# Gated attention products of batches 2 to 7 computed with the gated values stationary and 512 weight columns moving

## The chip, the cores and the metric

The kernel runs on one core of a Trainium2 chip. The time of a kernel is the device time of one execution in microseconds (us); a comparison takes the median of several. The five engines are called as the profile calls them: PE is TensorE (matmuls; PEld are its loads of the stationary operand), DVE is VectorE, ACT is ScalarE, POOL is GpSimd, and SP (SyncE) issues the transfers.

## What is computed

The reference, cut to its core:

```python
q_s = softmax of q over d;  k_s = softmax of k over s         # q, k, v: (8, 8, 576, 64)
kv = np.einsum('bhsd,bhse->bhde', k_s, v)
attn = np.einsum('bhsd,bhde->bhse', q_s, kv)
x = attn.transpose(0, 2, 1, 3).reshape(8, 576, 512)
gate_pre = sum(conv_w[k] * xp[:, k:k + S, :] for k in range(5))   # causal, along s
gate = 1.0 / (1.0 + np.exp(-gate_pre))
val = x @ w_val                                                # 512 x 512
return gate * val @ w_out                                      # 512 x 512
```

There are 8 batches of 576 tokens with 512 channels. The two products with the 512 x 512 weights, val and out, are most of the arithmetic.

## The kernel before

Everything of a batch lies with channels on the partitions, in four blocks of 128 channels, and with the 576 tokens as columns. A batch goes through these steps, each a function that the list ORDER calls by name with the batch and a block: the softmax of q and k (steps q_..., k_..., l_..., c_...), kv (L484), attend (L543: x, two blocks at a time), x_high and x_low (x as a sum of two fp32r parts), first, tap, far and near (the five taps of the convolution, on ACT, DVE, and POOL), sigmoid (L580), value (val), gated (L652: g = gate times val), g_high (gh, a rounded copy of g, L168 on ACT or L170 on POOL and DVE), g_low (gl = g - gh, L660, mostly on POOL), project (out), copy (half of out from the PSUM buffer to o, L174 on ACT or L178 on DVE) and put (L680: the transfer of o to memory).

ORDER has been written out by hand and is executed word for word (the schedule is manual): every engine gets its instructions in the order of the list, and only waits move them in time. Steps of neighbouring batches are interleaved; around the products of batch b stand the attend, taps and x parts of batch b+1 and the softmax of batches b+2 and b+3.

Value and project use split_product (L593). A step "project b n" makes output channels of block n: for each of the 4 input blocks there are three parts, gh with the low and the high half of the weights and gl with the high half; the weights' 128 x 128 block is stationary, and the tokens move in two halves of 288 columns. That is 12 parts x 2 halves = 24 matmuls, each with a load of weights. Of the block that gated made last, all three parts come at the end.

The PSUM holds four buffers of 128 x 1024 (tag "bank"), which x, val, out and others take in the order of the list; the first matmul into a buffer waits until its last reader is done. gh and gl have four buffers each, o has two.

Of the kernel before, what the change touches and what calls it, by code (L numbers as in the profile page):

```python
# [23 lines left out]
STAGED = 6  # L24
EPS = 1e-9
# [32 lines left out]
    q_turned 1 1 a, g_high 0 3 a, first 1 0 a, g_low 0 3 p, signed 6, load_k 2, first 1 1 a, tap 1 0 3, tap 1 0 1,
    load_q 3 0 5, tap 1 1 3, joined 6 p, project 0 1, x_high 1 0 a, w_high 6 a, tap 1 0 0, tap 1 1 0, copy 0 1 a a,
    k_spread 2, x_high 1 1 a, tap 1 0 2, q_sub 2 4 p, project 0 0, x_low 1 0, w_low 6 p, load_km 6 2, tap 1 1 1,  # L60
    put 0 1, attend 1 1, q_sub 2 3 p, copy 0 0 a a, part 7 a, tap 1 1 2, x_high 1 3 a, load_vt 2, signed 7,
    x_low 1 1, load_vt 4, q_sub 2 2 p, joined 7 p, first 1 2 a, q_sub 2 0 p, x_low 1 3, x_high 1 2 a, q_sub 2 1 p,
    load_km 4 1, project 0 2, far 1 2 2, x_low 1 2, load_km 4 2, w_high 7 a, load_v 2, w_low 7 p, tap 1 2 1,
    q_max 3 0 4, value 1 0, k_sub 2 1 p, q_sub 3 1 p, load_km 3 3, tap 1 2 3, k_sub 2 4 p, sigmoid 1 0, first 1 3 a,
    copy 0 2 a a, project 0 3, q_exp 2 0 5, gated 1 0, q_sum 2 0 5, k_peak 3 0, kt_exp 2, q_sub 3 0 p, q_eps 2 0 5 a,
    k_sub 2 3 p, tap 1 3 0, load_km 5 3, value 1 1, put 0 0, copy 0 3 a a, q_rec 2 0 5, k_sub 2 0 p, tap 1 3 2,
    tap 1 3 1, tap 1 3 3, k_sub 2 2 p, k_peak 3 3, q_mul 2 3 p, value 1 3, load_km 3 1, g_high 1 0 p, tap 1 2 0,
# [689 lines left out]
```

## Time and profile before

| | |
|---|---|
| median of 3 runs | 288.77 us (288.74 to 289.95) |
| span of the profiled execution | 287.3 us, 1.5 us below the median |
| busy PE | 267.8 us, 93% |
| busy DVE | 231.5 us, 81% |
| busy POOL | 206.2 us, 72% |
| busy ACT | 191.6 us, 67% |
| matmuls | 2616, of them 744 with 128 x 288 columns of out_a, and 24 of the two halves of the last product |

The span lies between the first and the last instruction; what the run has beside it, start and end, is the 1.5 us. Busy shares are averages over the whole span. The chain of waits goes back from the last instruction to what released each step; a step with a line and a count is so many instructions one behind the other on that engine. In a timeline each row is a start, a duration of the run of equal instructions, and the idle time before it where there was one. Matmuls overlap, so a group's mean duration is longer than their spacing.

### The profile page before, as it was taken

Reading aid. Unit: us, or ns where it says so; the run is one execution under the profiler, and the core shown is the slowest. Engines: PE = TensorE matmul, PEld = TensorE weight load, DVE = VectorE, ACT = ScalarE, POOL = GpSimd, SP = SyncE. Lnnn points to the kernel's source line nnn. Section 1 sums busy time; section 2 is a strip of 40 time slices with the busy share of each in tenths; the row PEclk is TensorE's granted clock in tenths of the full one; section 3 lists DMA queues with packets and bytes.
Section 4 is the critical chain, followed back from the end, with each engine's and each line's share of the span. In section 5 each row is a group of like instructions: output and inputs, shape, how many; then the busy total and the mean of one; then the engine's idle time right before and its main releaser. Section 6 shows DMA issues by size and latency. Waiting matters only on the chain.

```text
span 287.3 us, 6606 instructions
## 1 busy us (share of the span) xinstructions
PE 267.8 (93%) x2616; PEld 248.2 (86%) x2616; DVE 231.5 (81%) x332; ACT 191.6 (67%) x323; POOL 206.2 (72%) x187
## 2 busy tenths in 40 slices
PE   0198999999999999999999999999999999999995
PEld 0075799889998899889999898999989898989995
DVE  2999899999979999899669989799659774759610
ACT  2799999977797668856956773688945733645002
POOL 3767968989999986899898993879379193533300
PEclk9999999999999999999999999999999999999999
DMA  7999894598379899969997969645645700112022
GB/s 232 385 412 417 329 332 114 190 332 322 117 164 285 298 259 346 349 223 233 368 411 246 235 232 343 256 164 131 178 149 149 217 8 2 43 41 82 2 82 82
DMA packets 23462, 62.92 MB, mean 219 GB/s; under 512 B 3432, under 2 KB 3976, under 8 KB 20744
## 3 DMA queue, kind: packets, MB, share of 16 engines
q1 hardware_dynamic: 23432, 62.51, 65.5%
q8 instruction: 20, 0.33, 0.5%
q14 instruction: 10, 0.08, 0.1%
HBM read 52.96 MB, written 9.54 MB: 218 GB/s over the span
## 4 chain that ended last, share of the span: by engine, by line
PE 65%; DVE 13%; DMA 8%; POOL 6%; ACT 4%; issue 3%; SPq 0%; DVEq 0%; POOLq 0%; ACTq 0%
PE out_a L593 31%; PE val L593 25%; PE x L543 4%; DMA kc<-in_k_channels 4%; PE kv L484 3%; DMA kt<-in_k_tail 3%; POOL gl L660 2%; DVE gate L568 2%; DVE ktop L339 1%; ACT q L469 1%; DMA words<-in_w_val 1%; POOL q L471 1%; DVE g L652 1%; DVE e L263 1%; DVE qs L393 1%
## 5 line engine op out<-in xcount | busy, mean ns | idle before, releaser
L593 PE MATMUL val<-x,w_val_hi 128*128 128x288 f32 x512 | 89.0, 295 | 0.0
L568 DVE SCALAR_TENSOR_TENSOR gate<-x,cw,gate 128x575 f32<-128x575 f32 (+3 forms) x98 | 78.3, 808 | 4.8 <-ACT gate L556 1.9
L593 PEld LDWEIGHTS val<-x,w_val_hi 128*128 128x128 f32 x512 | 75.2, 188 | 0.1
L593 PE MATMUL val<-x,w_val_lo 128*128 128x288 f32 x256 | 56.0, 300 | 0.1
L593 PE MATMUL out_a<-gh,w_out_lo 128*128 128x288 f32 x248 | 54.6, 301 | 0.2 <-ACT far L573 0.2
L593 PE MATMUL out_a<-gh,w_out_hi 128*128 128x288 f32 x248 | 53.2, 296 | 0.0
L660 POOL TENSOR_TENSOR gl<-g,gh 128x576 fp32r<-128x576 f32 x25 | 36.1, 1443 | 13.8 <-ACT gh L168 6.5
L593 PEld LDWEIGHTS out_a<-gh,w_out_lo 128*128 128x128 f32 x248 | 39.3, 188 | 5.7 <-issue 2.2
L593 PE MATMUL out_a<-gl,w_out_hi 128*128 128x288 f32 x248 | 43.1, 295 | 0.3 <-POOL gl L660 0.3
L593 PEld LDWEIGHTS val<-x,w_val_lo 128*128 128x128 f32 x256 | 40.7, 188 | 1.4 <-issue 0.6
L577 POOL TENSOR_TENSOR gate<-gate,far 128x572 f32<-128x572 f32 (+3 forms) x22 | 29.0, 1320 | 16.4 <-DVE gate L568 8.1
L593 PEld LDWEIGHTS out_a<-gh,w_out_hi 128*128 128x128 f32 x248 | 39.8, 188 | 0.0
L383 POOL TENSOR_TENSOR q<-q,qm 128x512 f32<-128x512 f32 x32 | 32.9, 1044 | 6.3 <-DVE qm L378 6.3
L593 PEld LDWEIGHTS out_a<-gl,w_out_hi 128*128 128x128 f32 x248 | 36.4, 188 | 0.6 <-POOL gl L660 0.6
L174 ACT ACTIVATE o<-out_a 128x576 f32<-128x576 f32 x26 | 16.9, 651 | 29.3 <-PE out_a L593 22.6
L652 DVE SCALAR_TENSOR_TENSOR g<-gate,val 128x576 f32<-128x576 f32 x32 | 23.9, 750 | 15.4 <-PE val L593 10.1
L453 POOL TENSOR_TENSOR qc<-qc,lb 128x576 f32<-128x576 f32 (+1 forms) x17 | 24.3, 1439 | 10.8 <-DMA lb<-lrow 8.2
L318 POOL TENSOR_TENSOR k<-k,kmax 128x512 f32<-128x512 f32 x23 | 30.1, 1328 | 0.2
L580 ACT ACTIVATE gate<-gate 128x576 f32<-128x576 f32 x30 | 20.1, 682 | 8.6 <-DVE gate L568 7.1
L563 DVE TENSOR_TENSOR x<-x,x 128x576 fp32r<-128x576 f32 x32 | 23.2, 749 | 1.7 <-ACT x L168 1.6
L573 ACT ACTIVATE far<-x,cw 128x572 f32<-128x572 f32 (+3 forms) x22 | 16.2, 739 | 12.5 <-PE x L543 4.7
L168 ACT CAST x<-x 128x576 fp32r<-128x576 f32 x27 | 17.0, 640 | 7.3 <-PE x L543 4.2
(110 smaller groups left out, 441.2 us busy)
## 6 DMA issues: line engine op xcount, KB each, us to landing
out<-o SPq DMA_DIRECT2D x31, 288.0 KB, 3.9
v<-in_v SPq DMA_DIRECT2D x8, 1040.0 KB, 8.7
q<-in_q SPq DMA_DIRECT2D x7, 1024.0 KB, 8.6
km<-in_k_strided SPq DMA_DIRECT2D x24, 288.0 KB, 5.5
k<-in_k SPq DMA_DIRECT2D x6, 1024.0 KB, 8.5
qc<-in_q_channels SPq DMA_DIRECT2D x16, 288.0 KB, 7.7
lb<-lrow SPq DMA_DIRECT2D x8, 576.0 KB, 5.9
kc<-in_k_channels SPq DMA_DIRECT2D x8, 288.0 KB, 6.9
```

The costliest lines, as they stand in the source:

```text
L168: nc.scalar.copy(out=out, in_=in_)
L174: nc.scalar.mul(out, in_, factor)
L318: engine(e).tensor_sub(kk[r, cs], kk[r, cs], mx[r, cs])
L383: engine(e).tensor_tensor(qq, qq, m, op=ALU.add if b < 2 else ALU.subtract)
L453: engine(e).tensor_sub(t, t, T["lb", b][:, p])
L563: nc.vector.tensor_sub(xl, T["x", b, p], T["xh", b, p].bitcast(F32))
L568: nc.vector.scalar_tensor_tensor(out=a, in0=x, scalar=w, in1=a, op0=ALU.mult, op1=ALU.add)
L577: nc.gpsimd.tensor_add(a, a, T["far", b, p, j])
L580: nc.scalar.activation(T["gate", b, p], T["gate", b, p], AF.Tanh, scale=0.5)
L593: nc.tensor.matmul(ps[:, cs], a[:, kb, ms], z[:, cs], start=(i == 0), stop=(i == len(parts) - 1))
L652: nc.vector.scalar_tensor_tensor(out=T["g", b, m], in0=T["gate", b, m], scalar=1.0, in1=T["val", b, m], op0=ALU.add, op1=ALU.mult)
L660: engine(e).tensor_sub(T["gl", b, m], T["g", b, m], T["gh", b, m].bitcast(F32))
```

## The change

Batches 0 and 1 stay as they are. From batch 2 on (FIRST_TURNED) the product of project is made the other way round: 128 tokens of gh or gl are the stationary operand, and 512 columns of weights move, so that a step makes 128 tokens with all 512 output channels. Steps n = 0 to 3 are the first 512 tokens, with 12 matmuls of 512 columns instead of 24 of 288. The last 64 tokens of a batch go into a shared tile gt of its pair (batches 2 and 3, 4 and 5, 6 and 7): g_high and g_low copy and subtract them in an instruction of 64 columns of their own, while gh and gl have 512 columns now. A new step "project b 4" of the odd batch makes the product of the 128 tail tokens of the pair, again 12 matmuls, with a copy and a put of its own. The last product, project 7 3, stays split in two halves, now of 256 output channels. The output array is flat, its bytes are the same, and the host brings it into the reference's shape.

The functions:

```diff
     def g_high(b, m, e="a"):
-        T["gh", b, m] = block("gh", f"gh_{b}_{m}", 4, F32R)
-        copied(e, T["gh", b, m], T["g", b, m])
+        T["gh", b, m] = block("gh", f"gh_{b}_{m}", 4, F32R, columns(b))
+        copied(e, T["gh", b, m], T["g", b, m][:, :columns(b)])
+        if turned(b):
+            copied(e, g_tails(b)[:, 0, m, rows(b)], T["g", b, m][:, MAIN:])
 
     def g_low(b, m, e="p"):
-        T["gl", b, m] = block("gl", f"gl_{b}_{m}", 4, F32R)
-        engine(e).tensor_sub(T["gl", b, m], T["g", b, m], T["gh", b, m].bitcast(F32))
+        T["gl", b, m] = block("gl", f"gl_{b}_{m}", 4, F32R, columns(b))
+        engine(e).tensor_sub(T["gl", b, m], T["g", b, m][:, :columns(b)], T["gh", b, m].bitcast(F32))
+        if turned(b):
+            hi, lo = (g_tails(b)[:, i, m, rows(b)] for i in range(2))
+            engine(e).tensor_sub(lo, T["g", b, m][:, MAIN:], hi.bitcast(F32))
+
+    def turned(b):
+
+        return b >= FIRST_TURNED
+
+    def columns(b):
+        return MAIN if turned(b) else S
+
+    def g_tails(b):
+        if ("gt", b // 2) not in T:
+            t = pair(f"gt_{b // 2}", F32R, "late", 2)[:, :2 * NB * P]
+            T["gt", b // 2] = t.rearrange("p (i n s) -> p i n s", i=2, n=NB)
+        return T["gt", b // 2]
 
     def project(b, n, h="a"):
+        if turned(b):
+            return token_product(b, n, h)
         T["out", b, n, h] = halved_bank(f"out_{b}_{n}_{h}")
         split_product(T["out", b, n, h], W[1], blocks("gh", b), blocks("gl", b), n, T["gates", b], 1, h)
 
-    def piece(h):
+    def token_product(b, n, h="a"):
+
+        cs = piece(b, h)
+        ps = T["out", b, n, h] = bank(f"out_{b}_{n}_{h}")[:, :MAIN]
+        if n < 4:
+            hi, lo = ([t[:, n * P:n * P + P] for t in blocks(x, b)] for x in ("gh", "gl"))
+        else:
+            hi, lo = ([g_tails(b)[:, i, kb] for kb in range(NB)] for i in range(2))
+        wh, wl = W[1]
+        order = T["gates", b]
+        parts = []
+        for ks in (order[:NB - 1], order[NB - 1:]):
+            parts += [(hi[kb], w, kb) for kb in ks for w in (wl, wh)] + [(lo[kb], wh, kb) for kb in ks]
+        for i, (a, w, kb) in enumerate(parts):
+            nc.tensor.matmul(ps[:, cs], a, w[:, kb, cs], start=(i == 0), stop=(i == len(parts) - 1))
+
+    def piece(b, h):
+        if turned(b):
+            return cols(h)
         ts = tokens(h)
         return slice(ts[0].start, ts[-1].stop)
 
     def copy(b, n, h, e):
         if ("o", b, n) not in T:
             T["o", b, n] = block("o", f"o_{b}_{n}", 2)
-        cs = piece(h)
+        cs = piece(b, h)
         mid = (cs.start + cs.stop) // 2
         for i, k in enumerate(e):
             c = cs if len(e) == 1 else (slice(cs.start, mid), slice(mid, cs.stop))[i]
             times(k, T["o", b, n][:, c], T["out", b, n, h][:, c], 0.5)
 
     def put(b, n, h="a"):
-        nc.sync.dma_start(out=out[b, n][:, piece(h)], in_=T["o", b, n][:, piece(h)])
+        cs = piece(b, h)
+        to = out.rearrange("(t p j) -> t p j", p=P, j=C)[36 // 8 * b + b // 2 + n] if turned(b) else out.rearrange("(t p j) -> t p j", p=P, j=S)[b * NB + n]
+        nc.sync.dma_start(out=to[:, cs], in_=T["o", b, n][:, cs])
```

In ORDER steps are added and one is moved (put 3 1 stood before x_low 5 0). The list's lines are cut here to the steps around each place:

```diff
-    near 4 1 1, k_exp 5, k_peak 7 3, project 3 2, q_sub 6 3 p,
+    near 4 1 1, k_exp 5, k_peak 7 3, project 3 2, project 3 4, q_sub 6 3 p,
...
-    copy 3 2 a a, tap 4 2 2, put 3 2, l_sub 5 1 p, load_qc 6 1, kv 5,
+    copy 3 2 a a, tap 4 2 2, put 3 2, copy 3 4 a a, put 3 1, put 3 4, l_sub 5 1 p, load_qc 6 1, kv 5,
...
-    first 5 2 a, put 3 1, x_low 5 0,
+    first 5 2 a, x_low 5 0,
...
-    put 5 1, project 5 3, load_qc 7 0,
+    put 5 1, project 5 3, project 5 4, load_qc 7 0,
...
-    copy 5 3 a a, first 6 2 v, sigmoid 6 0, put 5 3, tap 6 2 3,
+    copy 5 3 a a, copy 5 4 a a, first 6 2 v, sigmoid 6 0, put 5 3, put 5 4, tap 6 2 3,
...
-    put 7 1, project 7 3 r, copy 7 2 a a, put 7 2, project 7 3 l,
+    put 7 1, project 7 4, project 7 3 r, copy 7 2 a a, copy 7 4 a v, put 7 2, put 7 4, project 7 3 l,
```

There are 744 + 24 matmuls of out before; of them 576 belong to batches 2 to 7, and 336 take their place. The 24 tail copies are on ACT (9), POOL (11) and DVE (4), the 24 tail subtractions on POOL (17) and DVE (7); there are three more copies of out (two on ACT, one on DVE) and three more puts.

On PE, the end of project 3 2 and the start of value 4 0, which comes behind it; before:

```order
L593 MATMUL out_3_2_a_2259<-gh_3_3_2119,w_out_lo_80 128x288 x2
L593 MATMUL out_3_2_a_2259<-gh_3_3_2119,w_out_hi_79 128x288 x2
L593 MATMUL out_3_2_a_2259<-gl_3_3_2125,w_out_hi_79 128x288 x2
L593 MATMUL val_4_0_2301<-x2_4_0_2121,w_val_lo_78 128x288 [waits DVE_49]
L593 MATMUL val_4_0_2301<-x2_4_0_2121,w_val_lo_78 128x288
L593 MATMUL val_4_0_2301<-x2_4_0_2121,w_val_hi_77 128x288 x2
L593 MATMUL val_4_0_2301<-x2_4_1_2204,w_val_lo_78 128x288 x2
L593 MATMUL val_4_0_2301<-x2_4_1_2204,w_val_hi_77 128x288 x2
```

and with the change:

```order
L702 MATMUL out_3_2_a_2192<-w_out_hi_79,gh_3_3_2086 128x512
L702 MATMUL out_3_2_a_2192<-w_out_hi_79,gl_3_3_2093 128x512
L702 MATMUL out_3_4_a_2205<-w_out_lo_80,gt_1_1498 128x512 [waits DVE_49,PE_49]
L702 MATMUL out_3_4_a_2205<-w_out_hi_79,gt_1_1498 128x512
L702 MATMUL out_3_4_a_2205<-w_out_lo_80,gt_1_1498 128x512
L702 MATMUL out_3_4_a_2205<-w_out_hi_79,gt_1_1498 128x512
L702 MATMUL out_3_4_a_2205<-w_out_lo_80,gt_1_1498 128x512
L702 MATMUL out_3_4_a_2205<-w_out_hi_79,gt_1_1498 128x512 x4
L702 MATMUL out_3_4_a_2205<-w_out_lo_80,gt_1_1498 128x512
L702 MATMUL out_3_4_a_2205<-w_out_hi_79,gt_1_1498 128x512
L702 MATMUL out_3_4_a_2205<-w_out_hi_79,gt_1_1498 128x512 [waits Pool_49]
L595 MATMUL val_4_0_2235<-x2_4_0_2089,w_val_lo_78 128x288 [waits Activation_49]
```

Twelve matmuls of 512 columns with the tail tile gt as stationary operand stand between the two products; the first of them waits for DVE, which val 4 0 did before, and val 4 0 waits for ACT.

On ACT, from the copy of out 3 1 (o_3_1) to the exp of q of batch 6; k5 is the exp of k, gate_4_0 and gate_4_1 are the two sigmoids; before:

```order
L174 ACTIVATE o_3_1_2254<-out_3_1_a_2207 128x576 [waits DMAHW7_49,PE_49,Activation_49]
L322 ACTIVATE k5_1883<-k5_1883 128x2048 [waits DMAHW0_49,Pool_49]
L168 CAST x2_4_3_2285<-x_4_3_2244 128x576 [waits PE_49]
L556 ACTIVATE gate_4_3_2293<-x_4_3_2244,cw_76 128x576
L580 ACTIVATE gate_4_0_2152<-gate_4_0_2152 128x576 [waits DVE_49]
L580 ACTIVATE gate_4_1_2191<-gate_4_1_2191 128x576 [waits DVE_49,Pool_49]
L174 ACTIVATE o_3_2_2329<-out_3_2_a_2259 128x576 [waits DMAHW2_49,PE_49,Activation_49]
L387 ACTIVATE q6_2044<-q6_2044 128x2560 [waits DMAHW0_49,Pool_49]
```

and with the change:

```order
L176 ACTIVATE o_3_1_2187<-out_3_1_a_2152 128x512 [waits DMAHW7_49,PE_49,Activation_49]
L324 ACTIVATE k5_1844<-k5_1844 128x2048 [waits DMAHW0_49,Pool_49]
L170 CAST x2_4_3_2219<-x_4_3_2177 128x576 [waits PE_49]
L558 ACTIVATE gate_4_3_2227<-x_4_3_2177,cw_76 128x576
L582 ACTIVATE gate_4_0_2109<-gate_4_0_2109 128x576 [waits DVE_49]
L582 ACTIVATE gate_4_1_2136<-gate_4_1_2136 128x576 [waits DVE_49,Pool_49]
L176 ACTIVATE o_3_2_2263<-out_3_2_a_2192 128x512 [waits DMAHW2_49,PE_49,Activation_49]
L176 ACTIVATE o_3_4_2267<-out_3_4_a_2205 128x512 [waits DMAHW4_49,PE_49,Activation_49]
L389 ACTIVATE q6_2007<-q6_2007 128x2560 [waits DMAHW0_49,Pool_49]
```

The copy of out 3 2 stands at the same place behind the exp and the two sigmoids, and the copy of out 3 4 comes behind it.

On POOL, the last gh and gl of batch 2 ahead of project 2 0; before:

```order
L170 CAST gh_2_3_1676<-g_2_3_1581 128x576 [waits DVE_49]
L660 TENSOR_TENSOR gl_2_3_1678<-g_2_3_1581,gh_2_3_1676 128x576 [waits PE_49,Pool_49]
L660 TENSOR_TENSOR gl_2_0_1700<-g_2_0_1549,gh_2_0_1673 128x576 [waits PE_49,Activation_49]
L170 CAST gh_2_2_1703<-g_2_2_1689 128x576 [waits DVE_49]
L660 TENSOR_TENSOR gl_2_2_1706<-g_2_2_1689,gh_2_2_1703 128x576 [waits PE_49,Pool_49]
L453 TENSOR_TENSOR qc_3_2_1543<-qc_3_2_1543,lb3_1448 128x512 [waits DMAHW5_49]
```

and with the change:

```order
L172 CAST gh_2_3_1680<-g_2_3_1584 128x512 [waits DVE_49]
L172 CAST gt_1_1498<-g_2_3_1584 128x64
L664 TENSOR_TENSOR gl_2_3_1683<-g_2_3_1584,gh_2_3_1680 128x512 [waits PE_49,Pool_49]
L667 TENSOR_TENSOR gt_1_1498<-g_2_3_1584,gt_1_1498 128x64 [waits Pool_49]
L664 TENSOR_TENSOR gl_2_0_1706<-g_2_0_1552,gh_2_0_1676 128x512 [waits PE_49,Activation_49]
L667 TENSOR_TENSOR gt_1_1498<-g_2_0_1552,gt_1_1498 128x64 [waits Activation_49]
L172 CAST gh_2_2_1710<-g_2_2_1695 128x512 [waits DVE_49]
L172 CAST gt_1_1498<-g_2_2_1695 128x64
L664 TENSOR_TENSOR gl_2_2_1714<-g_2_2_1695,gh_2_2_1710 128x512 [waits PE_49,Pool_49]
L667 TENSOR_TENSOR gt_1_1498<-g_2_2_1695,gt_1_1498 128x64 [waits Pool_49]
L455 TENSOR_TENSOR qc_3_2_1545<-qc_3_2_1545,lb3_1448 128x512 [waits DMAHW5_49]
```

Each gh and gl of 576 columns has become one of 512 and one of 64 on the shared tile gt.

## Rows read from the trace of the kernel before

**Rows 1.** The page: busy PE, and DVE and clock in 40 slices of 7.18 us.

```profile
PE 267.8 (93%) x2616; PEld 248.2 (86%) x2616; DVE 231.5 (81%) x332; ACT 191.6 (67%) x323; POOL 206.2 (72%) x187
...
DVE  2999899999979999899669989799659774759610
...
PEclk9999999999999999999999999999999999999999
```

**Rows 2.** Chain of waits from 118 us: start in us, length, engine and line.

```profile
121.74 1.44 POOL gl L660
...
123.22 3.73 PE out_a L593 x26
126.95 1.29 PE x L543 x16
128.23 6.59 PE out_a L593 x48
...
161.23 1.13 PE x L543 x16
162.37 3.39 PE out_a L593 x24
165.76 3.20 PE val L593 x24
...
182.55 3.20 PE out_a L593 x24
```

**Rows 3.** Groups by line, matmul and load: shapes, count, busy us, mean ns, idle.

```profile
L593 PE MATMUL out_a<-gh,w_out_lo 128*128 128x288 f32 x248 | 54.6, 301 | 0.2 <-ACT far L573 0.2
...
L593 PEld LDWEIGHTS out_a<-gh,w_out_lo 128*128 128x128 f32 x248 | 39.3, 188 | 5.7 <-issue 2.2 <-ACT o L174 1.8 <-DVE g L652 0.9
```

**Rows 4.** Timeline of PE: start, us, engine, line, tiles, shapes, count.

```profile
87.74 0.82 PE L509 MATMUL qTps<-ident,q 128*128 128x128 f32 x6
```

**Rows 5.** Timeline of DVE in 121 to 134.5 us.

```profile
125.33 1.65 DVE L568 SCALAR_TENSOR_TENSOR gate<-x,cw,gate 128x573 f32<-128x573 f32 x2
...
130.48 1.41 DVE L563 TENSOR_TENSOR x<-x,x 128x576 fp32r<-128x576 f32 x2
```

**Rows 6.** Timeline of DVE in 159 to 160 us.

```profile
159.10 1.53 DVE L568 SCALAR_TENSOR_TENSOR gate<-x,cw,gate 128x572 f32<-128x572 f32 x2
```

**Rows 7.** Timeline of ACT in 161.9 to 167 us.

```profile
161.99 1.92 ACT L322 ACTIVATE k<-k 128x2048 f32<-128x2048 f32 x1
...
164.97 1.26 ACT L580 ACTIVATE gate<-gate 128x576 f32<-128x576 f32 x2
```

**Rows 8.** Timeline of POOL in 158 to 166 us.

```profile
163.78 1.42 POOL L577 TENSOR_TENSOR gate<-gate,far 128x572 f32<-128x572 f32 x1
```

**Rows 9.** Timeline of DVE in 182 to 190 us.

```profile
184.84 2.81 DVE L412 TENSOR_REDUCE qs<-q 128x40 f32<-128x2560 f32 x1
...
188.95 0.80 DVE L568 SCALAR_TENSOR_TENSOR gate<-x,cw,gate 128x573 f32<-128x573 f32 x1
```

**Rows 10.** Timelines of DVE and PE at the end of batch 7.

```profile
272.71 0.76 DVE L660 TENSOR_TENSOR gl<-g,gh 128x576 fp32r<-128x576 f32 x1
...
274.09 0.43 PE L593 MATMUL out_a<-gl,w_out_hi 128*128 128x288 f32 x2
```

**Rows 11.** Groups by line of small and large operations, columns as in rows 3.

```profile
L660 POOL TENSOR_TENSOR gl<-g,gh 128x576 fp32r<-128x576 f32 x25 | 36.1, 1443 | 13.8 <-ACT gh L168 6.5 <-DVE gh L170 4.5 <-DVE lse L423 1.9
...
L469 ACT ACTIVATE q<-q,qs 128x64 f32<-128x64 f32 x40 | 10.1, 335 | 0.4 <-DVE qs L406 0.3
...
L291 POOL TENSOR_TENSOR w_out_lo<-f,w_out_hi 128x512 fp32r<-128x512 f32 x4 | 5.1, 1290 | 0.0
...
L698 POOL MEMSET ones<- 128x64 f32 x1 | 0.2, 152 | 0.0
```

**Rows 12.** Timeline of the sync queue in 166 to 189 us.

```profile
167.23 0.37 SPq L216 DMA_DIRECT2D qc<-in_q_channels  x1
...
188.00 0.43 SPq L680 DMA_DIRECT2D out<-o  x1
```

More of the change, by code (lines that the diff above doesn't have):

```diff
@@ L58 @@
[L58 to L67, printed above, removed]
@@ new lines @@
+    put 0 2, x_high 2 1 a, q_total 3, first 2 0 a, first 2 1 a, q_log 3, q_turned 2 1 v, g_high 1 2 p, g_low 1 2 p,
+    project 1 3, tap 2 1 1, project 1 0, tap 2 1 2, tap 2 0 3, x_low 2 1, load_km 5 1, load_q 4 0 5, copy 1 3 a v,
+    k_row 4, k_sub 3 2 p, k_sub 3 1 p, near 2 1 0, far 2 1 3, attend 2 1, near 2 1 3, l_turn 3, copy 1 0 a a,
+    k_peak 5 0, first 2 3 a, x_high 2 2 a, l_row 3, tap 2 0 1, tap 2 0 2, k_sub 3 3 p, x_low 2 0, q_max 4 0 5,
+    k_sub 3 0 p, first 2 2 a, put 1 3, put 1 0, far 2 0 0, load_v 4, k_sub 3 4 p, load_qc 3 0, project 1 2,
@@ new lines @@
+    k_peak 7 1, l_sub 5 3 p, load_k 6, k_spread 6, tap 4 3 1, sigmoid 4 2, tap 4 3 0, attend 5 0, gated 4 2,
+    value 4 1, l_sub 5 2 v, first 5 1 a, load_q 7 0 5, x_high 5 0 a, tap 5 1 3, load_v 6, sigmoid 4 3, tap 5 1 2,
+    g_high 4 2 v, tap 5 1 1, g_low 4 2 p, value 4 3, gated 4 1, x_high 5 1 a, g_high 4 1 p, x_low 5 1, tap 5 1 0,
+    g_low 4 1 p, c_exp 5 2, c_exp 5 3, gated 4 3, first 5 0 a, far 5 0 3, g_high 4 3 a, g_low 4 3 v, project 4 0,
+    far 5 0 0, near 5 0 3, near 5 0 0, q_total 6, attend 5 1, copy 4 0 a a, k_sub 6 1 p, put 4 0, project 4 2,
@@ new lines @@
+    k_sub 7 0 p, first 6 0 a, project 5 0, copy 5 2 a a, l_sub 6 2 v, kt_exp 7, put 5 2, l_spread 7, tap 6 0 3,
+    k_sub 7 1 p, tap 6 0 2, k_sub 7 3 p, project 5 1, tap 6 0 1, copy 5 0 a a, c_exp 6 2, x_low 6 0, put 5 0,
+    near 6 0 0, tap 6 1 2, tap 6 1 1, tap 6 1 0, attend 6 1, copy 5 1 a a, put 5 1, project 5 3, project 5 4,
+    load_qc 7 0, x_high 6 2 a, x_high 6 3 v, far 6 2 2, k_sub 7 2 v, first 6 3 a, x_low 6 1, x_low 6 2, l_sub 7 3 p,
+    x_low 6 3, value 6 1, sigmoid 6 1, tap 6 3 3, copy 5 3 a a, copy 5 4 a a, first 6 2 v, sigmoid 6 0, put 5 3,
@@ new lines @@
+    copy 6 1 a v, tap 7 1 3, put 6 1, x_low 7 0, near 7 1 2, near 7 0 2, far 7 0 1, tap 7 1 1, project 6 3,
+    copy 6 0 a a, tap 7 1 0, put 6 0, near 7 0 1, far 7 0 0, near 7 0 0, attend 7 1, copy 6 3 a v, x_low 7 1,
+    project 6 2, x_high 7 3 a, first 7 2 a, x_high 7 2 a, x_low 7 2, x_low 7 3, sigmoid 7 1, value 7 2, tap 7 2 3,
+    copy 6 2 a a, tap 7 2 2, put 6 2, put 6 3, first 7 3 v, far 7 2 1, tap 7 3 3, near 7 2 1, value 7 1, tap 7 3 2,
+    tap 7 2 0, far 7 3 0, sigmoid 7 2, tap 7 3 1, sigmoid 7 0, gated 7 2, near 7 3 0, value 7 0, g_high 7 2 a,
@@ L755 @@
     got = r.results[0]["out_0"]
[L756 removed]
+    got = got.reshape(B // 2, 2, S * C)
+    n = FIRST_TURNED
+    early = got.reshape(B, C, S)[:n].transpose(0, 2, 1)
+    late = got.reshape(B // 2, 2 * S, C)[n // 2:]
+    main, tails = late[:, :2 * MAIN].reshape(-1, MAIN, C), late[:, 2 * MAIN:].reshape(-1, D, C)
+    return np.concatenate([early, np.concatenate([main, tails], axis=1)])
```

151 lines of the change are left out of this document (71 added, 80 removed).

## The prediction

> **What bounds the kernel now.** I read the page first: TensorE (PE) is busy for 267.8 of 287.3 us, at a granted clock of nine tenths or more in every slice, the higher of its two levels, 2.4 GHz [rows 1]. Then I read the chain of waits: its last step on another engine is the GpSimd subtraction gl at 121.74, and from 123.22 to 284.1 it is PE alone [rows 2]. So every nanosecond that PE saves after 123 us counts, as long as nobody else becomes late; and VectorE (DVE) is at eight or nine tenths up to 201 us and has gaps only after that [rows 1]. That is the question of this case: what do the turned products save on PE, and who is behind PE by how much.
>
> **The price of a product.** A product of 24 matmuls of 288 columns takes 3.20 us, and 3.39 when it follows an attend [rows 2]; 3.20/24 = 133.3 ns each, which is 320 clocks of 2.4 GHz for 288 columns. The record of a matmul (301 ns) is longer than its spacing, since they overlap, and a weight load of 188 ns lies beside each [rows 3]. The changed product has 12 matmuls of 512 columns, also with a load each, and no row shows that length. From both sides: one column a clock and nothing else is 213.3 ns; the same cost per column as now is 133.3 x 512/288 = 237.0 ns. In between, if the 32 clocks over 288 belong to each matmul with its load and not to each column, it is 213.3 + 13.3 = 226.7 ns. I take 226.7, since every matmul on both sides has a load of the same 128x128 size, and the excess is a whole 32 clocks. A product then takes 12 x 0.2267 = 2.72 us, 0.48 less than 3.20.
>
> One row speaks for less: six transposes in a row, each with a 128x128 load of its own, take 0.82 us to the end of the last, whose record is 0.273; (0.82 - 0.273)/5 = 109 ns for 128 columns, two clocks a column and 2.5 ns over [rows 4]. There the load costs nearly nothing. But that operand moves at half the pace, so a load could share what the stream leaves free; it is not the nearest row.
>
> The Trainium skill, "TensorE: Matmul & The Clock Gate", section "Back-to-back issue gap", gives the isolated gap at full clock as N/2.4 + 2.5 ns: 122.5 for 288 columns, where this trace has 133.3, and 215.8 for 512; by it a product would take 2.59. The same section gives some 131 ns for 512 columns in a sustained stream, and the row of 133.3 for only 288 columns speaks against that. The first is rival A's price, which stands by itself on the transposes.
>
> **PE's sum.** 24 main products lose 0.48 each: -11.52. The tail products 3 4, 5 4 and 7 4 are new, 2.72 each: +8.16. The last product is split into two halves of 256 columns; 24 matmuls of 106.7 + 13.3 = 120 ns are 2.88 instead of 2.72: +0.16. Net -3.20 us. The change so removes 72 columns of each product of 576 and gives three eighths of a product per batch back; an even batch gains 1.92, an odd one loses 0.80.
>
> **What of it is kept.** PE gains only where the engine it waits for next is early enough.
>
> *Batch 2.* Project 2 0 ends on gl 2 2 of GpSimd, which ends at 121.74 + 1.44 = 123.18, with PE going on at 123.22 [rows 2]. That chain starts from DVE and ScalarE, not from PE, so all of this product's 0.48 is lost. Is it later by the new tail operations? The 512-column subtraction is cheaper: 1443 ns for 576 columns, 1290 for 512 [rows 11], -0.15. A 64-column GpSimd operation is bounded by the memset's 152 ns below and by 1443 x 64/576 + the memset = 0.31 above; I take 0.22, so a pair costs +0.07, and the shorter gh gives about that back: zero. Next, attend 3 1 overwrites the tile that the taps of gate 3 1 read; the two taps at 125.33 end at 126.98, with PE's attend at 126.95 [rows 2, 5]: project 2 1 keeps nothing. Project 2 2's gain goes to the wait of project 2 3 for the first of the two x_low at 130.48, whose tile it takes over, and which ends at 131.19 [rows 5], and PE was to start there at 128.23 + 3.39 = 131.62, by the chain [rows 2]: of these 0.43 I take 0.2 as kept (0.13 is my allowance for every handover, and the start of a matmul by the chain is up to 0.15 late). With project 2 3's own 0.48 the lead at val 3 0 (128.23 + 6.59 = 134.82) is 0.68. Lost: 1.92 - 0.68 = 1.24.
>
> *Attend 4 1* comes after three products of batch 3, which gain 1.44. It waits for the last tap of gate 4 0, the first of the two at 159.10, ending at 159.9 [rows 6]; before, PE came at 161.23 [rows 2]. That is 1.32 behind DVE, less 0.13 for the handover: lost 0.25.
>
> *The tail product 3 4 and val 4 0.* Project 3 4 takes the buffer that val 4 0 had, and val 4 0 takes that of out 3 2, so it now waits for copy 3 2 on ScalarE. PE gets there at 165.76 + 2.72 - 0.68 - 1.19 - 0.48 = 166.13. Copy 3 2 stands behind the exp of 161.99, x_high, first and the two tanh at 164.97 [rows 7], the second of which waits for GpSimd's addition, 163.78 + 1.42 = 165.20 [rows 8]. With 0.13 handover, half of 1.26 for the tanh and some 0.59 for a 512-column copy it ends at 166.5 if GpSimd does not move with PE's lead and at 166.0 if it does; I take the middle and a handover: lost 0.25 (0 to 0.5). Behind val 4 0 the whole of PE is queued. After batches 2 and 3 PE is 0.62 later than before.
>
> *Batch 4.* Project 4 1 takes the buffer of x 5 0, read by the DVE tap that starts at 188.95 and ends at 189.75, after the reduce of 2.81 at 184.84 [rows 9]. PE was at that point about 190.1 (the two products begin at 186.88, from 182.55 + 3.20 + 1.13 [rows 2]), 0.37 behind DVE. Two shorter products would bring it 0.96 earlier, DVE's new tail subtraction in front of the reduce (its smallest operations are some 0.15) pushes the other way: 0.23 is kept. Lost 0.73.
>
> *Batches 5 to 7.* DVE has gaps here [rows 1], and I find at least 1 us before each wait of PE on it: nothing lost in 5 and 6. At the end, gl 7 3 ends on DVE at 272.71 + 0.76 = 273.47 and is needed at 274.09 [rows 10]; the nine matmuls ahead of it now cover 2.04 instead of 2.40 and gl is loaded as weights: 0.1.
>
> Small operations elsewhere: 24 tail copies (ScalarE 9, GpSimd 11, DVE 4) and 24 tail subtractions (GpSimd 17, DVE 7). A 64-column ScalarE operation is 335 ns [rows 11]; nine of them add some 2.5 us to an engine at 67%. They hide behind the products, except as counted. On the sync queue, put 3 1 moves from 188.00 to ahead of the load at 167.23 [rows 12], with put 3 4 behind it waiting for copy 3 4; the loads behind may start up to 1 us later, and are wanted some 40 us later: nothing. If that cover were gone it would cost that 1 us.
>
> **Sum.** -3.20 + 1.24 + 0.25 + 0.25 + 0.73 + 0.10 = -0.63 us, on the span of 287.3; the 1.5 us between it and the median of 288.77 are start and end, which stay. Forecast: 288.1 us.
>
> **Rivals.** *A, the load is hidden entirely.* A matmul is 213.3 + 2.5 = 215.8 ns as in the transposes, a product 2.59. PE's sum is -24 x 0.61 + 3 x 2.59 + 0.03 = -6.84; the losses grow with the lead, since the others don't move: batch 2 1.64, attend 4 1 0.7, val 4 0 0.6, batch 4 1.0, end 0.2, together 4.14. Net -2.7: 286.1 us. For it: the row of transposes; against it: the 133.3 ns, where the load was beside the stream as well.
>
> *B, the cost belongs to the columns* (237 ns, product 2.84). It ends on the other side. A pair of batches has the same columns as before, so PE's sum is zero: -0.36 for each main product, +2.84 for each tail product. But the gains come in batch 2, where DVE and GpSimd hold PE (0.86 of 1.44 lost), and the price in batch 3. With 0.48 at batch 4 and 0.1 at the end: +1.4, 290.2 us. It decides from 231 ns a matmul on: each ns moves PE's sum by 12 x 21 = 0.25 us. For it: nothing in the rows parts columns from matmuls. Against it: 320/288 clocks a column would be an odd pace.
>
> *C, the others bound the even batches altogether.* With 226.7 ns, but the 1.92 of batch 6 lost as well, because DVE at nine tenths around 215 to 222 and 258 to 266 us [rows 1] is the bound there; the odd batches then still pay: -0.63 + 1.9 = 290.0 us. Against it: the slices between have 4 to 7 tenths.
>
> That the products would not be turned, or that the scheduler reorders them, is no case: the steps are executed in the list's order.
>
> **Chances.** Forecast 0.42, A 0.28, B 0.14, C 0.10, something else 0.06. A difference of 0.5%, 1.44 us, is what a measurement of this kernel can tell from none: faster is below 287.3, slower above 290.2. The forecast case has 0.09 faster (losses at their lower ends), 0.29 same, 0.03 slower; A 0.27 faster, 0.01 same; B and C half same, half slower (0.12 each); the rest is spread. That makes faster 0.37, same 0.44, slower 0.19. The range runs from A with somewhat smaller losses, 285.3, to 290.4, just above B. The likeliest one alone: 287.1 to 289.3.
>
> **What would show it.** In the profile after, a run of 512-column matmuls gives the pace: 12 in 2.72 us for the forecast, 2.59 for A, 2.84 for B. In the waits of PE there should be new ones: project 2 0 on gl, attend 3 1 and 4 1 on gate, val 4 0 on ScalarE's copy of out 3 2, project 4 1 on gate; each with the size above. After project 6 3, PE should have its largest lead, and C is right if it waits for DVE between 210 and 260 us. I am wrong if 512 columns go at a pace outside 213 to 237 ns, if a small 64-column operation costs much more than 0.3 us on a waiting engine, or if the three tail products wait for their own tile's last subtraction.

## The result and the profile after

| | before | after |
|---|---|---|
| median of 20 runs | 288.75 us (287.96 to 289.95) | 290.33 us (288.58 to 291.85) |
| ratio | | 1.0053 (95% interval 1.0036 to 1.0070) |
| span of the profiled execution | 287.3 us | 288.3 us |

The turned products make the kernel slower by half a per cent, where 0.2% faster was forecast. It is close to rival B of the prediction (290.2 us); the price of a matmul is the main cause, and how far B's number is luck is said at the end. The profiled execution of the changed kernel took 290.73 us, 2.4 more than its span, and over its 20 runs this remainder was 1.8 to 3.1 us, median 2.0; every other kernel below has 1.8 in the median, those with the same puts too. So some 0.2 us of the 1.58 between the medians lies beside the span; no run looked into that.

The page of the changed kernel, the lines that answer to [rows 1]. PE does 240 matmul instructions less and is busy for only 0.7 us less; DVE's slices change little and the clock's not at all:

```profile
PE 267.1 (93%) x2376; PEld 232.4 (81%) x2376; DVE 233.9 (81%) x344; ACT 192.5 (67%) x334; POOL 209.9 (73%) x215
...
DVE  1999999999979998999669969799969764758700
...
PEclk9999999999999999999999999999999999999999
```

The chain of waits of the changed kernel answers to [rows 2] (start in us, length, engine and line, count). Read two things in it: 12 matmuls behind other products take 2.81 us, not 2.72, and the stretches of batch 2 and batch 4 now come from DVE (a tap, "gate"), where before the chain went from POOL's gl into the products of batch 2 [rows 2] and was PE alone in batch 4:

```profile
126.25 0.83 DVE gate L570
...
127.21 1.20 PE x L545 x16
128.41 3.00 PE out_a L702 x12
...
131.46 3.04 PE out_a L702 x12
134.49 6.40 PE val L595 x48
...
159.74 1.18 PE x L545 x16
160.92 5.82 PE out_a L702 x24
166.73 3.20 PE val L595 x24
...
185.93 2.73 DVE qs L414
188.66 0.72 DVE gate L570
...
190.04 0.73 DVE gate L570
...
190.82 3.06 PE out_a L702 x12
193.88 3.21 PE val L595 x24
197.08 2.81 PE out_a L702 x12
```

The waits of PE (us in total, times, longest) tell the same. The kernel before waited 0.3 us for gl at a product of out, and at no attend for a tap:

```profile
PE out_a L593 <- POOL gl L660: 0.3, 1, 0.3
```

The changed kernel waits 0.6 for gl, and there are new waits for a tap, at an attend (batch 3's second) and at a product (project 4 1):

```profile
PE x L545 <- DVE gate L570: 0.7, 1, 0.7
...
PE out_a L702 <- POOL gl L664: 0.6, 1, 0.6
...
PE out_a L702 <- DVE gate L570: 0.3, 1, 0.3
```

The chains of both kernels side by side, each the start of the step in us:

| step | before | after | after - before |
|---|---|---|---|
| attend 3 1 | 126.95 | 127.21 | +0.26 |
| value 3 0 | 134.82 | 134.49 | -0.33 |
| attend 4 1 | 161.23 | 159.74 | -1.49 |
| value 4 0 (in after behind project 3 4) | 165.76 | 166.73 | +0.97 |
| value 5 1 | 193.48 | 193.88 | +0.40 |
| kv 6 | 206.28 | 206.29 | +0.01 |
| value 6 1 (in after behind project 5 4) | 227.60 | 228.88 | +1.28 |
| project 7 0 | 271.32 | 271.04 | -0.28 |
| end of the last product | 284.11 | 285.11 | +1.00 |

The even batches give, the odd ones take, as the prediction had it; but batch 4 gives only 0.96 (from +0.97 to +0.01) where batch 6 gives 1.56 (from +1.28 to -0.28), and batches 3, 5 and 7 take 1.3 each.

### The profile page after: what moved, and what is told of

Same layout as the page of the kernel before. It is cut to its first block, busy times and chain, and to the rows that moved or that the text cites. A ratio compares the mean times of both kernels' runs of the same rounds, so it can differ in the third digit from the quotient of the medians.

```text
span 288.3 us, 6196 instructions
## 1 busy us (share of the span) xinstructions
PE 267.1 (93%) x2376; PEld 232.4 (81%) x2376; DVE 233.9 (81%) x344; ACT 192.5 (67%) x334; POOL 209.9 (73%) x215
## 4 chain that ended last, share of the span: by engine, by line
PE 60%; DVE 15%; DMA 12%; ACT 5%; POOL 4%; issue 3%; SPq 0%; DVEq 0%; POOLq 0%
PE val L595 25%; PE out_a L702 22%; PE out_a L595 5%; DMA lb<-lrow 4%; PE x L545 4%; DMA kc<-in_k_channels 4%; PE kv L486 3%; DVE gate L570 3%; DMA out<-o 2%; DVE ktop L341 2%; DMA words<-in_w_val 1%; ACT q L471 1%; DVE x L565 1%; POOL q L473 1%; DVE qm L380 1%
## 5 line engine op out<-in xcount | busy, mean ns | idle before, releaser
L664 POOL TENSOR_TENSOR gl<-g,gh 128x512 fp32r<-128x512 f32 (+1 forms) x25 | 34.2, 1368 | 12.5 <-DVE gt L172 6.6
L702 PE MATMUL out_a<-w_out_lo,gh 128*128 128x512 f32 x92 | 37.6, 408 | 0.4 <-DVE gate L570 0.3
L702 PE MATMUL out_a<-w_out_hi,gh 128*128 128x512 f32 x92 | 36.4, 396 | 0.0
L176 ACT ACTIVATE o<-out_a 128x512 f32<-128x512 f32 (+1 forms) x28 | 17.1, 610 | 28.6 <-PE out_a L702 16.5
L455 POOL TENSOR_TENSOR qc<-qc,lb 128x576 f32<-128x576 f32 (+1 forms) x17 | 23.7, 1405 | 10.9 <-DMA lb<-lrow 10.9
L702 PE MATMUL out_a<-w_out_hi,gl 128*128 128x512 f32 x92 | 29.1, 397 | 0.6 <-POOL gl L664 0.6
L702 PEld LDWEIGHTS out_a<-w_out_lo,gh 128*128 128x128 f32 x92 | 17.3, 188 | 8.7 <-ACT o L176 1.3
L702 PEld LDWEIGHTS out_a<-w_out_hi,gl 128*128 128x128 f32 x92 | 17.3, 188 | 5.4 <-POOL gl L664 1.0
L380 DVE TENSOR_REDUCE qm<-q 128x8 f32<-128x512 f32 (+3 forms) x12 | 20.8, 1742 | 0.0
```

Source lines behind the costliest of these rows:

```text
L380: nc.vector.tensor_reduce(out=T["qm", b][:, cs], in_=qq, axis=AX.X, op=ALU.max, negate=b < 2)
L455: engine(e).tensor_sub(t, t, T["lb", b][:, p])
L664: engine(e).tensor_sub(T["gl", b, m], T["g", b, m][:, :columns(b)], T["gh", b, m].bitcast(F32))
L702: nc.tensor.matmul(ps[:, cs], a, w[:, kb, cs], start=(i == 0), stop=(i == len(parts) - 1))
```

## The experiments

Every kernel but those with appended series was timed in turn with the kernel before on the same chip; a ratio is to that. Two theories stood against each other after the result. W: the 512-column matmul costs 234 ns, so PE saves only 0.9 us in all, and the others (DVE above all) take what it saves in batches 2 and 4. T: every pair of batches pays for its tail product and its small operations.

### What a matmul costs

The series stand behind the last product; nothing else runs there, and the granted clock is 1.00. The edit (shapes in the order of the series; n moving columns, m stationary ones; "b" is bf16, "f" the weights stationary, "s" each matmul a sum of its own):

```diff
+    def pace(v):
+        n, m, kind = [(64, 128, "r"), (128, 128, "r"), ..., (288, 128, "f"), (512, 128, "k")][v]
+        ps = bank(f"pace{n}x{m}{kind}_")
+        gs, w = [blocks("gh", 7)[i] for i in range(NB)], W[1][0]
+        for i in range(17):
+            a, z = gs[i % NB][:, (i // NB % 4) * P:(i // NB % 4) * P + m], w[:, i % NB, :n]
...
+            nc.tensor.matmul(ps[:m, :n], a, z, start=(i == 0 or kind == "s"), stop=(i == 16 or kind == "s"))
```

> The changed kernel with 17 series of 17 matmuls appended behind the last product, whose results are not used, so its own time says nothing. They give the spacing of matmuls on a full clock: fp32r operands with 64 to 512 moving columns and a 128-column stationary operand; 288 and 512 columns with a 64-column stationary operand; 288 and 512 columns each started anew instead of accumulated; 256 and 512 columns in bf16; 288 columns with the weights stationary; 512 columns with the same stationary block each time. In the changed kernel 12 matmuls of 512 columns take 2.81 us (234 ns) and 12 of 256 columns 1.41 (118 ns). Theory P (the excess belongs to the 4-byte moving columns, about 1.09 to 1.11 clocks each): spacing goes in proportion to columns from 192 up, 88 at 192, 118 at 256, 133 at 288, 176 at 384, 234 at 512; the 64-column load changes nothing; bf16 gives 213 to 216 at 512. Theory L (the load of the stationary operand takes time from the stream): a 64-column load brings 512 columns nearer to 216 to 225 and 288 nearer to 122 to 127, and bf16 with the same 128-column load keeps an excess. Below some 192 columns both expect the load to set the spacing, at about 107 to 115 ns.

The timeline of PE in this kernel (start in us, length of the whole series, shapes, count); the next row's start gives the 17 spacings:

```profile
285.16 2.09 PE L718 MATMUL pace128x128r__3558<-w_out_hi,gh 128*128 128x128 f32 x17
...
289.01 2.18 PE L718 MATMUL pace256x128r__3594<-w_out_hi,gh 128*128 128x256 f32 x17
291.03 2.42 PE L718 MATMUL pace288x128r__3612<-w_out_hi,gh 128*128 128x288 f32 x17
...
298.74 3.56 PE L718 MATMUL pace448x128r__3666<-w_out_hi,gh 128*128 128x448 f32 x17
302.14 4.14 PE L718 MATMUL pace512x128r__3684<-w_out_hi,gh 128*128 128x512 f32 x17
...
308.35 4.03 PE L718 MATMUL pace512x64r__3720<-w_out_hi,gh 128*64 128x512 f32 x17
...
320.31 3.83 PE L718 MATMUL pace512x128b__3795<-pb 128*128 128x512 bf16 x17
```

From start to start within a series, from its second matmul to its last (the first step differs in some): 111.7 ns at 64, 128 and 192 columns, 117.3 at 256, 132.8 at 288, 147 at 320, 174 at 384, 200 at 448, 234 at 512; with a 64-column stationary operand 132 at 288 and 227 at 512; started anew each time 132 and 234, with one stationary block for all 234; with the weights stationary 132 at 288. In bf16, with a 128-column load: 109.2 at 256 and 215.8 at 512. So it is not the side that is stationary. A bf16 stream takes 2.5 ns over one column a clock, and a 4-byte stream has an excess of 11 ns at 256 columns, 13 to 14 from 288 to 448 and 21 at 512. This goes more with theory P than with L, but it does not part the load from the stream: the record of a bf16 load is 98 ns long and that of a 4-byte load 188, and the 64-column load did take 7 ns off at 512. Nor is P's proportion strict: at 448 columns the excess was 13.3, as the fixed 32 clocks of the prediction would have it, and only at 512 more. The second series looked there.

> Again the changed kernel with series of 17 unused matmuls behind the last product (its own time says nothing). The first series gave an excess over one column a clock of 12.9 ns at 288 columns, 13.3 at 448, 20.5 at 512, 13.3 at 512 with a 64-column stationary operand, and 2.5 in bf16. Theory F (a fixed excess of some 13 ns of a 4-byte matmul, plus at 512 columns a further 7 that belongs to the full 128-column load): 464 to 496 columns rise from 13 to 20 or keep 13 until the last; 512 columns with 32 and 64 stationary columns keep about 13; 448 and 288 columns keep 12 to 13 with 32 stationary columns. Theory L (all of the excess is the load's): with 32 stationary columns 512 comes to 216 to 219 ns, 448 to 190, 288 to 122 to 125. 64 partitions instead of 128, the low half as the stationary operand, and the weights stationary with gated values moving should change nothing by either.

The timeline of PE in the second one:

```profile
287.36 3.67 PE L720 MATMUL pace448x128r__3558<-w_out_hi,gh 128*128 128x448 f32 x17
...
301.97 4.14 PE L720 MATMUL pace512x128r__3630<-w_out_hi,gh 128*128 128x512 f32 x17
...
309.87 4.09 PE L720 MATMUL pace512x64r__3666<-w_out_hi,gh 128*64 128x512 f32 x17
313.80 4.08 PE L720 MATMUL pace512x32r__3684<-w_out_hi,gh 128*32 128x512 f32 x17
```

448 columns now took 206.5 ns where the same instructions had taken 200, and 512 columns with 64 stationary ones 231 where they had taken 227. With 96, 64 and 32 stationary columns 512 cost 231, far from the 216 to 219 of theory L, which falls, though the record of a 32-column load is only 108 ns long. Theory F falls too: 512 columns with a narrow load do not keep 13 ns, and 448 columns have no fixed price. 464, 480 and 496 columns (212, 217 and 223 ns) lie 17 to 19 ns over one column a clock. Within a series the spacing wanders (226 to 235 with 32 stationary columns), and one series with weights on both sides went from 231 to 226 halfway. What stays is a band: a 4-byte stream of 256 to 512 columns takes 1.06 to 1.11 clocks a column, and where in the band it lies depends on something that these series don't show. In the kernel 288 columns lie at 1.11 and 512 at 1.10, so turning saves hardly anything per column. What shifts the spacing within the band is left open.

### Which batches lose

> Only batches 4 to 7 turned; batches 2 and 3 as before, put 3 1 at its old place. PE's sum with 2.81 us a product: 16 x -0.39 + 2 x 2.81 + 0.02 = -0.60. Theory W (the loss is that of waits in batch 2, 1.2 us, and batch 4, some 0.6): batch 4's loss stays, net about 0: 288.75 us, ratio 1.000. Rival T (each pair pays a third, by its tail product and its small operations): two thirds of the measured 1.5 remain: 289.8 us, ratio 1.0035.

```diff
-FIRST_TURNED = 2
+FIRST_TURNED = 4
```

(with project 3 4, its copy and its put left out, and put 3 1 at its old place). Measured: 288.72 us, ratio 1.0006 (0.9984 to 1.0028). Theory W had 288.75.

> Only batches 6 and 7 turned. PE's sum: 8 x -0.39 + 2.81 + 0.02 = -0.29. Theory W: no wait of PE in these batches, the whole is kept: 288.45 us, ratio 0.999. Rival T: one third of the 1.5 us remains: 289.25 us, ratio 1.0018.

The same with FIRST_TURNED = 6: 288.44 us, ratio 0.9985 (0.9965 to 1.0006); W had 288.45, T 289.25. Timed once more:

> The same kernel as with batches 6 and 7 alone turned, timed again since its interval of 0.9965 to 1.0006 held 1. Theory W: PE's sum of -0.29 us is kept in full: ratio 0.999. Rival T: 1.0018.

288.41 us, ratio 0.9992 (0.9973 to 1.0011). Both times the median is 0.3 us below that of before, PE's sum for one pair, but the intervals hold 1, so a version that is shown to beat the kernel before is not among these.

> The changed kernel without the 64-column copies and subtractions of the tails; the tail products stay, with the first 128 tokens of the odd batch in place of the tail tile, so the tails' outputs are left out. PE's work is that of the changed kernel. Theory W (batch 2 cannot keep its gain, whatever the small operations cost): 0.2 to 0.5 us come back, in batches 2 and 4: about 290.0 us. Rival O (the small operations on GpSimd, VectorE and ScalarE make the waits): 1.0 to 1.5 us come back: 288.8 to 289.3 us.

```diff
-        if turned(b):
-            copied(e, g_tails(b)[:, 0, m, rows(b)], T["g", b, m][:, MAIN:])
...
-            engine(e).tensor_sub(lo, T["g", b, m][:, MAIN:], hi.bitcast(F32))
...
-        if n < 4:
-            hi, lo = ([t[:, n * P:n * P + P] for t in blocks(x, b)] for x in ("gh", "gl"))
-        else:
-            hi, lo = ([g_tails(b)[:, i, kb] for kb in range(NB)] for i in range(2))
+        hi, lo = ([t[:, n % 4 * P:n % 4 * P + P] for t in blocks(x, b)] for x in ("gh", "gl"))
```

Measured: 290.24 us, ratio 1.0048 (1.0031 to 1.0065): 0.1 us comes back of the 1.5, and behind value 3 0 the trace is 0.03 us shorter. By the intervals up to 0.8 us could come back, but not the 1.0 to 1.5 of rival O. The small operations are not the cause, though some are dearer than estimated. The groups by line of the changed kernel have them (count, busy us, mean ns):

```profile
L667 POOL TENSOR_TENSOR gt<-g,gt 128x64 fp32r<-128x64 f32 x17 | 6.1, 356 | 0.0
...
L667 DVE TENSOR_TENSOR gt<-g,gt 128x64 fp32r<-128x64 f32 x7 | 4.0, 565 | 0.0
...
L172 POOL CAST gt<-g 128x64 fp32r<-128x64 f32 x11 | 2.6, 240 | 0.0
```

The mean of 565 ns on DVE comes from two of the seven: five took 0.21 to 0.34 us, those at 205.38 and 266.98 took 1.44 and 1.31. Each of these two started while a subtraction of POOL ran, and ended 0.08 us behind its end. PE waited for neither.

### Is PE the bound in batch 2, and in batch 6?

The reverse of a gain: PE gets as much more work as the turned products save there, and somewhat over.

```diff
+            for _ in range(2 if b == 2 and i == 0 else 0):
+                nc.tensor.matmul(ps[:, cs], a, w[:, kb, cs], start=True, stop=True)
             nc.tensor.matmul(ps[:, cs], a, w[:, kb, cs], start=(i == 0), stop=(i == len(parts) - 1))
```

> The changed kernel with the first matmul of each of the four products of batch 2 done three times: 8 more matmuls of 512 columns, 8 x 0.234 = 1.87 us more for PE there, somewhat over the 1.56 that the turned products save in batch 2. Theory W (up to value 3 0 the others set the pace, PE has nothing to gain there): little of it shows, 0.3 to 0.6 us over the changed kernel's 290.33: ratio 1.006 to 1.008. Rival (PE sets the pace in batch 2 as well, the loss has another place): +1.87: 292.2 us, ratio 1.012.

Measured: 290.33 us, ratio 1.0063 (1.0040 to 1.0086): 0.3 us over the changed kernel by the ratios (with an error of some 0.8), nothing by the medians, for 1.87 us of work. The rival's ratio of 1.012 lies outside the interval. The chain of its profile shows the attend of batch 3 still behind the same tap of DVE, ahead of the last two products of batch 2, with the extra matmuls as rows of their own (x2):

```profile
126.00 0.83 DVE gate L570
...
126.96 1.20 PE x L545 x16
128.16 0.66 PE out_a L703 x2
128.82 2.81 PE out_a L704 x12
```

> The same with batch 6: 8 more matmuls, 1.87 us, where no row shows PE waiting. Theory W: all of it shows, 290.33 + 1.87 = 292.2 us, ratio 1.012, which says that batch 6 kept its 1.56. Rival C of the prediction (VectorE bounds the even batches, batch 6 too): 0.9 us or less shows: at most 291.2 us, ratio below 1.009.

With b == 6: 291.88 us, ratio 1.0105 (1.0069 to 1.0142), 1.5 us over the changed kernel. The interval is wide, but the chain has nothing but PE from the attend to the values of batch 7, each extra pair in full length:

```profile
244.03 1.13 PE x L545 x16
245.16 0.66 PE out_a L703 x2
245.82 2.81 PE out_a L704 x12
248.62 0.47 PE out_a L703 x2
...
255.18 1.13 PE x L545 x16
```

All traces together say it most clearly. Cut each at the first matmul of value 3 0:

| kernel | from value 3 0 to the end, us | median less that, us |
|---|---|---|
| before | 152.59 | 136.2 |
| changed | 154.01 | 136.3 |
| turned from batch 4 | 152.67 | 136.1 |
| turned from batch 6 (two profiles) | 152.32, 152.33 | 136.1, 136.1 |
| without the small tail operations | 153.98 | 136.3 |
| 8 more matmuls in batch 2 | 154.01 | 136.3 |
| 8 more matmuls in batch 6 | 155.93 | 136.0 |
| turned from batch 4, taps first (below) | 153.37 | 135.8 |
| before, tokens in 320 and 256 (below) | 152.64 | 135.9 |

Behind value 3 0 the length repeats within 0.03 us for the same work, and follows PE: 1.92 for the 1.87 of extra work. Ahead of it (with the start and end of the run), all kernels need 135.8 to 136.3, whether batch 2 is turned, not turned, or turned with extra work. These numbers are good to a few tenths only: the kernel before had 288.4 us beside the last four kernels of the table but 288.7 to 288.8 beside the others, and with the ratio in place of the median the extra work in batch 2 comes to 136.6.

It does not follow that PE has slack in batch 2. In the profile of before PE waits there for gl, but that is one execution. With batches 4 to 7 turned, batch 2 is as before, and the chain is PE alone from attend 3 0 to value 3 0 and for 6 us ahead of it:

```profile
117.98 1.13 PE x L540 x16
119.11 6.59 PE out_a L590 x48
125.70 1.13 PE x L540 x16
126.83 6.59 PE out_a L590 x48
```

In four of the six profiles with batch 2 unturned PE does not wait in this stretch at all, and it takes 15.34 to 15.36 us from matmul to matmul; the other two have 15.5 and 16.1 (before). With batch 2 turned the five profiles without extra work have 14.7 to 15.7, mean 15.2, with waits of PE for gl, for the tap, or for ACT's copy of out, twice behind a transfer of out; with the extra work it is 16.4. So 0.2 to 0.3 of the 1.56 us arrives on average: unturned, PE sets the time there, but the others end so close behind that nearly all of the gain is lost to them. And attend 3 0 itself starts anywhere from 117.9 to 119.7 us in these profiles, so the scatter lies ahead of it and hides a gain of this size in the medians.

### Can batch 4's loss be moved out of the way?

> Batches 4 to 7 turned as before, and VectorE's tap 5 0 2, x_low 5 0 and tap 5 0 1 moved ahead of the 2.81 us reduce (q_total 6), with GpSimd's addition near 5 0 0 behind them, so that the PSUM buffer which project 4 1 takes is free some 2.5 us earlier. Theory W: project 4 1 no longer waits, 0.5 us of batch 4 come back: 288.2 us, ratio 0.998, and in the trace the stretch from attend 5 0 to value 5 1 takes 17.4 us (before 18.55, with batches 4 to 7 turned 17.98). Rival: the wait only moves on, to VectorE's x_low for value 5 1: 288.7 us, ratio 1.0005, and the stretch from attend 5 0 to kv 6 keeps its length.

```diff
-    far 5 0 0, near 5 0 3, near 5 0 0, q_total 6, attend 5 1,
+    far 5 0 0, near 5 0 3, tap 5 0 2, x_low 5 0, tap 5 0 1, near 5 0 0, q_total 6, attend 5 1,
```

Measured: 289.16 us, ratio 1.0022 (1.0004 to 1.0039), where it was 1.0006 without the move; the intervals overlap, but from value 3 0 to the end the trace has 153.37 us, 0.70 more than without the move. The wait has moved on, as the rival said: in the chain DVE is without a pause from the first tap to the x_low of value 5 1, and PE, which no longer waits at project 4 1, waits there:

```profile
186.01 2.73 DVE qs L409
188.73 2.19 DVE qm L375
...
193.66 1.43 DVE x L560 x2
...
195.13 0.53 PE val L590 x2
```

From matmul to matmul project 4 2 and 4 1 take 5.72 us instead of 6.31 (0.59 back), and value 5 1 takes 4.53 instead of 3.20 (1.33 lost). The size of the loss has another cause than the order of DVE's own steps. Two small operations (lse) behind the reduces take 0.75 and 1.05 us, and on POOL larger ones run beside them:

```profile
190.84 0.75 DVE L420 TENSOR_TENSOR lse<-qm,qs 128x32 f32<-128x32 f32 x1
191.49 1.05 DVE L422 TENSOR_TENSOR lse<-qm,qs 128x8 f32<-128x8 f32 x1
```

```profile
190.06 1.45 POOL L574 TENSOR_TENSOR gate<-gate,far 128x575 f32<-128x575 f32 x1
191.45 4.07 POOL L380 TENSOR_TENSOR q<-q,qm 128x512 f32<-128x512 f32 x4
```

Each ends within 0.08 us of the end of the POOL operation beside it (191.51, and 192.52 for the first of the four). Without the move POOL is idle there until 190.64, and the same two take 0.21 and 0.16 us:

```profile
190.47 0.21 DVE L420 TENSOR_TENSOR lse<-qm,qs 128x32 f32<-128x32 f32 x1
```

The two slow subtractions of the tails above behave in the same way. From the first lse to the start of the x_low behind it 2.82 us pass instead of 1.37, which is more than the 1.33 lost. An estimate from these rows: without it x_low would have come 1.4 us earlier, and PE's wait of 0.67 us for it at 194.47 would be gone. Counted from attend 5 0, the move puts near 5 0 0 on POOL 2.4 us later, and with it the addition that stands at 190.06; an order that avoids this was not tried.

### Does the curve of the series pay elsewhere?

> The kernel before, unturned, with its tokens split in 320 and 256 columns instead of 288 and 288. The appended series gave 147.0 ns for 320 columns and 117.4 for 256, together 264.4, against 133 + 133 = 266. Theory P (the spacing follows this curve in the kernel as well): 12 x 1.8 ns a product less, 64 products, 1.4 us of PE; where PE sets the pace (from batch 3 on, about five eighths) it is kept: 0.8 us, 287.9 us, ratio 0.997. Rival: attend and the waits take it, or the difference of series does not carry over: 288.7 us, ratio 1.000.

```diff
-HALF = S // 2
+HALF = 320
...
-        return bank(name)[:, 512 - HALF:512 + HALF]
+        return bank(name)[:, 512 - HALF:512 - HALF + S]
```

Measured: 288.50 us, ratio 0.9995 (0.9973 to 1.0018), and from value 3 0 to the end 152.64 us, as before. The three products at the end take the same time as two halves of 288 did:

```profile
271.16 9.60 PE out_a L593 x72
```

Alternating, 320 columns cost 147.8 ns and 256 cost 118.8, together the 266.6 of 288 + 288. The small gains and losses within the band of the series depend on the sequence, and do not carry over.

## Why the prediction was wrong

**The price of a product: the step that failed.** The prediction took 226.7 ns a matmul because the excess at 288 columns is a whole 32 clocks. That was a coincidence of one length; 512 columns take 234.2 (2.81/12), near the upper bound of 237. A main product so saves 0.39 instead of 0.48, and each tail product costs 2.81 instead of 2.72. PE's sum is 24 x -0.39 + 3 x 2.81 + 0.02 = -0.91 us instead of -3.20. These 2.3 us make up the distance between forecast (-0.63) and result (+1.58), for the losses came out much as forecast in sum: 2.57 forecast, and some 2.2 in the runs (1.56 at most in batch 2, 0.05 at attend 4 1, 0.59 in batch 4). -0.91 + 2.2 is +1.3; the traces show +1.42 behind value 3 0 and nothing clear of the scatter ahead of it. Both bounds of the price were named; the choice between them had no row behind it. Before had no second length of an fp32r stream beside a 128x128 load, so a choice by "whole clocks" was worth less than it looked, and B's chance of 0.14 was too low.

Three readings beside it were off, without a term hanging on them. Each ns of the price moves PE's sum by 12 x 26 = 0.31 us and not by 12 x 21: 23 main products and three tail products are made of 512-column matmuls. A turned product loses 64 columns of 576, not 72, and a pair takes 128 back, half a product per batch. And DVE is not at eight or nine tenths throughout up to 201 us: [rows 1] has six tenths from 136 to 151 and seven from 79 to 86 and from 180 to 187.

The transposes, the row that spoke for rival A, do not show what was read from them. Their 109 ns may be two clocks a column, but the series of 64, 128 and 192 columns, each with a 128-column load, all took 111.7: beside such a load the spacing stays near this number however few the columns are, and what sets it is open. So 109 ns at 128 columns says little of the stream's price. That the width of the load matters little beside a long stream is shown by the second series instead (231 ns with 32 stationary columns, 234 with 128). The isolated gap of the Trainium skill, "TensorE: Matmul & The Clock Gate", section "Back-to-back issue gap", N/2.4 + 2.5 ns, holds to the nanosecond for the bf16 series (215.8 at 512, 122.5 at 288) and for none of the 4-byte series (234 and 133); for this kernel the measurement decides.

**Batch 2.** Right in kind for two of three waits: gl and the tap of gate 3 1 were named as what ends last, and they show in the waits and in the chain. For x_low at project 2 3 the trace shows only that this product took 3.04 us instead of 2.81, with no wait put down to DVE. Too good in size: 0.68 of 1.92 was to be kept; in the profile it is 0.33 of 1.56, and the medians show none of it. The wait for gl, from which the working started, stands in the profile of before but in none of the other five with batch 2 unturned; the reading rested on one execution, and what holds in all is that the others end close behind PE there.

**Attend 4 1 and value 4 0.** Losses of 0.25 each were forecast; the chain shows 0.05 (attend 1.18 instead of 1.13) and none (project 3 2 and 3 4 in 5.82 us, 3.00 + 2.81). The three products ahead of attend 4 1 gain 1.16 with the price measured, and the forecast had 1.19 free: with the smaller gain PE hardly reaches these waits.

**Batch 4.** Right in place and mechanism (the DVE taps behind the reduce hold the buffer of project 4 1), 0.59 lost where 0.73 was forecast. That another order would give it back was not claimed; the one that was tried did not, for the collision with POOL, and whether another would stays open.

**Batches 5 to 7.** Right: three products 8.63 instead of 9.79 in 5 and 6, nothing lost. Rival C fell with the extra work in batch 6, by the trace (1.92 us more for 1.87 of work); the interval of the times alone would still allow it. The 0.1 at the end is not there.

**The small operations** were thought to cost nothing, and they do (0.1 us), though a POOL subtraction of 64 columns is 356 ns and not 220, and two of DVE's, put at some 0.15 us, took 1.31 and 1.44. This sign of being wrong did come, on engines for which PE did not wait.

**Rival B** gave 290.2 us against 290.33 measured, and the price was nearly right with 237 for 234.2. That the totals agree to 0.1 us is luck: its PE's sum was zero for -0.91, and its losses were 1.44 for some 2.2 (batch 2 0.86, batch 4 0.48, end 0.1), two errors that cancel in part; some 0.2 us lies beside the span.

## What to carry to other kernels

A price for a shape that the trace does not have is to be kept as a range, and the forecast made for both ends, above all when one end has the other sign; a neat number of clocks at one length is no evidence for another length. A gain on an engine counts only up to the next engine behind it: here a sixth of the turned products stood in a stretch where the others end just behind PE and kept 0.2 to 0.3 of 1.56 us, while the price for them, the tail product, stood in one where PE alone sets the time and is paid in full. How much is free there is not read from one profile: the wait that the forecast started from stood in one of six. Adding work to an engine in one stretch tells whether it sets the time there, as far as the scatter of the runs allows; the trace of the stretch tells it more finely.
